# Symmetric transform matrices used as they are, a ring of three modulation tiles, and weight-gradient copies on one engine, in a spectral block's forward and backward pass

## The chip, the cores and the metric

The kernel runs on one core of a Trainium2 chip. A core has TensorE (PE in the profile; PEld is its weight load), VectorE (DVE), ScalarE (ACT), GpSimd (POOL) and SyncE (SP), each with an instruction queue of its own, and 16 DMA engines that all queues share. The metric is device microseconds of the whole execution, the median of several runs. A second, profiled execution gives the busy times and waits. In it, "SPq" and "POOLq" are the instructions with which SyncE and GpSimd start DMA transfers.

## The reference

One token sequence x of 2048 rows and 1024 columns passes two residual branches, each scaled and shifted by a modulation vector computed from a conditioning vector c. All outputs of the forward pass and of its gradient are wanted, ten arrays in all.

```
mod = (silu(c) @ w_mod).reshape(c.shape[0], 6, 1, -1)     # sa, ca, ga, sb, cb, gb
h = layernorm(x) * (1 + ca) + sa
x = x + ga * irfft2(rfft2(h) * (w_r + 1j * w_i))
h = layernorm(x) * (1 + cb) + sb
x = x + gb * (gelu(h @ w1 + b1) @ w2 + b2)
# and the gradients of x, w_r, w_i, w1, b1, w2, b2, c and w_mod for a given grad_out
```

w1 is 1024 by 3584, w2 is 3584 by 1024, and w_mod is 1024 by 6144. All is bfloat16. The gradient of w_mod is an outer product: each 128 by 1024 block of it is one row of the modulation gradient times a column of silu(c). The gradient of c needs the sum of each block of w_mod times that row.

## The kernel before

The two-dimensional transform is done as matmuls with cosine and sine matrices, folded by symmetry into four classes: even and odd cosines (`CE`, `CO`) and even and odd sines (`SE`, `SO`). The matrices are generated once in `gen_mats` and stored in DRAM: `d_SF` for the token axis, `d_E` for the column axis. `spectral_core` does one transform, the multiplication by the weights and the inverse transform. It runs twice, forward and backward (`fwd` is true and false). Its stages are:

- `s_fwd`: four passes with `pu` matmuls along tokens, giving `U`.
- eight pairs (`pair`, L473): `pcs` matmuls along columns, then VectorE products with the frequency weights `ws`, giving `R`. Backward, each pair also writes a piece of the weight gradients (out_2, out_3).
- `s_inv`: `pv` matmuls with the transposed token matrices `smi`, giving `V`.
- `po` matmuls with the transposed column matrices `gm`, whose result goes through `consume`.

The transposed matrices are fetched by transposing DMA transfers from DRAM: `load_smi` (L555) makes eight for each parity of frequency, and L576 to L581 make eight for `gm`. They are started on SyncE's queue during the first three pairs.

Between the two transforms lie the two layers of the mixer. `ph_part` (L661) computes `pp`, the gradient before the activation, and stores it in `d_ph`. `z_block` (L750) handles four 128-row pieces of the hidden layer for one of four token chunks, 28 blocks in all. It loads a piece of `d_ph` into `ph`, computes `pz` with TensorE, moves it out with ScalarE (L767), and runs the chain of the activation and its derivative over the tiles `zb`, `av`, `bv`, `sg`. Two sets of these tiles alternate from block to block (`gts`). The block ends with a multiply that also sums (L784), whose product is stored to `d_gz` (L786). `bo_pass` (L791) multiplies the hidden values by `w2` between the blocks, in an order written out in `plan`, and adds column sums to `gacc` (L825 to L828).

Then comes the gradient through w1 (`pg`, L956) with two layernorm backward steps, and the backward transform. Beside the backward transform TensorE computes the weight gradients. `pieces` (L1072) is a generator: each step is 16 matmuls for a 128 by 512 block (`gw2acc` for w2, `gw1acc` for w1) and a copy of the PSUM block into `gwo` or `gwo1` (L1054, L1120), then a store. Four `fill(1)` calls stand beside each pair, and others are in `consume_bwd` (L1018). `nc.any.tensor_copy` leaves it to the planner whether ScalarE or VectorE makes the copy.

The modulation gradients (`gmod_steps`, L894) go row by row, eight steps for each of six rows. Each step loads a block of w_mod into `wr`, forms the outer product in `gw` (L899) and stores it, then multiplies and sums `wr` (L901). Row 5 runs in the stage of `pg`, with two load tiles and one store tile. Rows 3 and 4 run beside the backward pairs, with one load tile and one store tile. Rows 2, 1 and 0 run at the end.

`consume_bwd` reloads a part of x (`load_tok`, partly by indirect transfers on GpSimd's queue) and normalizes it with four ScalarE instructions (`norm_act`, L440).

Instructions are traced in the order of the program, and a planner orders each engine's queue by priority and by what it expects to be ready. `tc.high_priority()` moves instructions forward, and `tc.issue_after(x)` keeps those of a block behind x on the same engine. On the chip each queue is worked off in that order, and an instruction at its head that waits holds those behind it.

Of the kernel before, what the change touches and what calls it, by code (L numbers as in the profile page):

```python
# [11 lines left out]
BF16 = mybir.dt.bfloat16  # L12
I32 = mybir.dt.int32
ACT = mybir.ActivationFunctionType
ALU = mybir.AluOpType
AX = mybir.AxisListType

P = 128
S = 2048
D = 1024  # L20
# [15 lines left out]
def kernel(  # L36
# [74 lines left out]
    d_P = dram.tile([8, P, 4 * PW], BF16, name="d_P")  # L111
    d_SF = dram.tile([P, 4, 4, 512], BF16, name="d_SF")
    d_E = dram.tile([P, 2, 8, 256], BF16, name="d_E")
    d_gmod = dram.tile([6 * D], BF16, name="d_gmod")
# [341 lines left out]
    def spectral_core(fwd, fb, sms, em, css, pt, evac_u, evac_c, evac_v, consume, o4tag, pfs=None, fill=lambda n: None, mid=lambda: None, beside=lambda n: None):  # L456
# [97 lines left out]

        def load_smi(par):  # L555
            smi = reg.tile([P, 2, 4, 512], BF16, name="smi", tag=("sma", "smb")[par])
            for t in range(2):
                for i in range(4):
                    with tc.issue_after(ld_in[0].ins):
                        nc.sync.dma_start_transpose(out=smi[:, t, :, i * P:(i + 1) * P], in_=d_SF[:, par + 2 * t, i, :])  # L560
            smis.append(smi)

        pair_load(0)
        for par in range(2):
            for m in range(4):
                if par == 1 and m == 2:
                    s_inv(CE, smis[0])
                    s_inv(SE, smis[0])
                pair(par * 4 + m, par, m)
                if par * 4 + m < 7:  # L570
                    pair_load(par * 4 + m + 1)
                beside(par * 4 + m)
                if par == 0 and m < 2:
                    load_smi(m)
                if par == 0 and m == 2:
                    gm = reg.tile([P, 12, 256], BF16, name="gm", tag="gm")  # L576
                    for cl in range(4):
                        for h in range(2):
                            with tc.issue_after(ld_in[0].ins):
                                nc.sync.dma_start_transpose(out=gm[:, 2 * cl:2 * cl + 2, h * P:(h + 1) * P],  # L580
                                                            in_=d_E[:, 0 if fwd else 1, 2 * cl + h, :])  # L581
        s_inv(CO, smis[1])
# [167 lines left out]
    def z_block(b, g0, g1):  # L750
# [3 lines left out]
        for g in range(g0, g1):  # L754
# [27 lines left out]
            for k in range(4):  # L782
                fc = g * 4 + k
                nc.vector.tensor_tensor_reduce(out=av[:, k, :], in0=ph[:, k, :], in1=av[:, k, :], scale=1.0, scalar=0.0,  # L784
                                               op0=ALU.mult, op1=ALU.add, accum_out=gb1_acc[:, fc, b:b + 1])
            nc.gpsimd.dma_start(out=d_gz_v[:, g * 4:(g + 1) * 4, b * BW:(b + 1) * BW], in_=av)  # L786

# [3 lines left out]
    def bo_pass(b, h):  # L791
# [30 lines left out]
        for i in range(4):  # L822
            with ordered():
                last_pe[0] = nc.tensor.matmul(pa[:], lhsT=ones_bf[:], rhs=go[:, i, :], start=(i == 0), stop=(i == 3))
        if b == 0:  # L825
            nc.vector.tensor_copy(out=gacc[:, cs_], in_=pa[0:1, :])
        else:
            tt(gacc[:, cs_], gacc[:, cs_], pa[0:1, :], ALU.add)  # L828

# [64 lines left out]
    def gmod_steps(r, wrs, gws, gr):  # L894
        nc.sync.dma_start(out=gr, in_=d_gmod[r * D:(r + 1) * D].partition_broadcast(P))
        for jc in range(NDC):
# [6 lines left out]
            yield  # L903

    w1Ts = []
    for g in range(7):
# [15 lines left out]
    gmg = reg.tile([P, 2, D], BF16, name="gmg", tag="sb")  # L922
    early = gmod_steps(5, gmw[:], gmg[:, 0:1], gmg[:, 1, :])
    au = reg.tile([P, 4, D], BF16, name="au", tag="px1")
# [12 lines left out]
    for b in range(NB):  # L937
# [26 lines left out]
        for i in range(4):  # L964
            t = 4 * b + i
            ln_bwd(gn3[:, i, :], sums[:, 0, i:i + 1], n3u[:, i, :], stats[:, 2, 0, t:t + 1], gn3[:, i, :], got[:, 4 + i % 2, :])
        tt(pru, gn3[:], n2u[:], ALU.mult)
        g2, ftmp = gn3, pru
# [5 lines left out]
        for i in range(4):  # L974
            t = 4 * b + i
            nc.vector.tensor_tensor_reduce(out=g2[:, i, :], in0=gn3[:, i, :], in1=opcb_row, scale=1.0, scalar=0.0,
                                           op0=ALU.mult, op1=ALU.add, accum_out=s2c[:, i:i + 1])
            ln_bwd(g2[:, i, :], s2c[:, i:i + 1], n2u[:, i, :], stats[:, 1, 0, t:t + 1], g2[:, i, :], got[:, 4 + i % 2, :])
        tt(g2[:], g2[:], go4, ALU.add)
        nc.gpsimd.dma_start(out=chunk_rows(d_gx1, b), in_=g2[:])  # L980
# [5 lines left out]
        if b < NB - 1:  # L986
            sums3_ga(b, au)
            for _ in range(3):
                next(early, None)

# [15 lines left out]
    pfs = [empf[:, 2048:2048 + 4 * PW].rearrange("p (s r w) -> p s r w", s=2, r=2), pf1[:]]  # L1006
    otl = reg.tile([P, 2 * NT * P + D], BF16, name="otl", tag="ot")
    hht = [reg.tile([P, 2, NT, P], BF16, name=f"hht{k}", tag=f"t{k + 2}") for k in range(2)]
    gmy = otl[:, NT * P:2 * NT * P].rearrange("p (a d) -> p a d", d=D)
    sacc = otl[:, 2 * NT * P:2 * NT * P + D]  # L1010
# [7 lines left out]
    def consume_bwd(i, o4, tmp, tmp2, n1):  # L1018
# [7 lines left out]
        load_tok(n1, A_x, i)  # L1026
        norm_act(n1, n1, 0, i)
        tt(tmp, o4, n1, ALU.mult)
# [8 lines left out]
        store_tok(out_1, o4, i)  # L1037
        fill((6, 6, 8, 8)[i])
        for q in range(4):
# [6 lines left out]
    gwo = reg.tile([P, 2, D], BF16, name="gwo", tag="ph")  # L1046

    def gw2_mm(acc, fc, h, t):
        nc.tensor.matmul(acc[:], lhsT=hh_s[hh_o[fc]][:, t, :], rhs=gBs[t // 4][:, t % 4, h * KH:(h + 1) * KH],  # L1049
                         start=(t == 0), stop=(t == NT - 1))  # L1050

    def gw2_out(acc, fc, h):
        with tc.high_priority():
            nc.any.tensor_copy(out=gwo[:, fc % 2, h * KH:(h + 1) * KH], in_=acc[:])  # L1054
        if h == 1:
            nc.gpsimd.dma_start(out=out_6[fc * P:(fc + 1) * P, :], in_=gwo[:, fc % 2])
# [15 lines left out]
    def pieces():  # L1072
# [36 lines left out]
        for fg in range(F // 512):  # L1109
            if fg < 6:  # L1110
                w1g["ins"] = gw1_load(fg + 1)
            gz2 = w1g["gz"][2 * (fg % 2):2 * (fg % 2) + 2]
            for cch in range(NDC):
                acc = ps_f("gw1acc")
                for t in range(NT):
                    nc.tensor.matmul(acc[:], lhsT=n3ns[t // 4][:, t % 4, cch * P:(cch + 1) * P], rhs=gz2[t // 8][:, t % 8, :],  # L1116
                                     start=(t == 0), stop=(t == NT - 1))
                ob = gwo1[:, (fg * NDC + cch) % 8]
                with tc.high_priority():
                    nc.any.tensor_copy(out=ob, in_=acc[:])  # L1120
                nc.gpsimd.dma_start(out=out_4[cch * P:(cch + 1) * P, fg * 512:(fg + 1) * 512], in_=ob)
                yield
# [25 lines left out]

    rows34 = [gmod_steps(r, gmy[:, 0:1], gmy[:, 1:2], sacc) for r in (3, 4)]
    side = [0]  # L1150

    def beside_bwd(n):
        for k in range(4):
            fill(1)
            if k < (0, 2, 2, 2, 2, 2, 3, 3)[n]:
                with tc.issue_after(hh_in[0].ins):
                    next(rows34[side[0] // NDC])
                side[0] += 1

# [58 lines left out]
```

## Time and profile before

The time is 1582.85 us, the median of 3 runs (1582.29 to 1590.55). The profiled run has a span of 1578.6 us.

| stage (us from start) | TensorE busy | granted clock | DMA share |
|---|---|---|---|
| 348 to 567, hidden blocks, first part | 191.0 of 219 | 0.94 | 0.68 |
| 567 to 817, hidden blocks, second part | 240.7 of 250 | 0.97 | 0.87 |
| 817 to 1044, gradient through w1 | 215.5 of 227 | 0.99 | 0.54 |
| 1133 to 1324, backward pairs | 160.0 of 191 | 0.93 | 0.79 |
| 1324 to 1428, inverse transform and x gradient | 100.9 of 104 | 1.00 | 0.67 |
| 1428 to 1545, weight gradient of w1 | 117.0 of 117 | 1.00 | 0.91 |

A stage's busy time is the time in which an engine had an instruction in work. The granted clock is the share of full speed that TensorE was given. The DMA share is the mean busy share of the 16 DMA engines.

In the lines of the prediction, a line of the timeline has start, duration, engine, line and operation, the tiles written and read, a count, and in brackets the idle time before it and what ended it. A line of the waits names who waited for whom, then microseconds in total, times, and the longest.

### The profile page before, as it was taken

The page shows a single profiled execution, that of the slowest core. Times are in us where ns is not written, and L with a number is a line of the kernel's source. Part 1 is how long each engine was busy: PE and PEld are TensorE (multiplying, and loading weights), DVE is VectorE, ACT ScalarE, POOL GpSimd, SP SyncE. Part 2 cuts the span into 40 slices and gives each one's busy share as a digit, 9 for nine tenths or more (in the row PEclk, how much of TensorE's full clock was granted, in tenths as well). Part 3 has the DMA queues.
Part 4 walks back from the last instruction along what each step waited for, and adds up shares of the span by engine and source line. Part 5 has one row for each costly group of instructions (what it writes and reads, how often), then busy time and mean ns, then how long its engine had stood idle before and what let it go on. Part 6 is the DMA issues. An engine that isn't in the chain of part 4 may idle for free.

```text
span 1578.6 us, 18397 instructions
## 1 busy us (share of the span) xinstructions
PE 1449.7 (92%) x6831; PEld 669.1 (42%) x6831; DVE 1074.5 (68%) x1578; ACT 722.3 (46%) x955; POOL 366.7 (23%) x427
## 2 busy tenths in 40 slices
PE   5989899999797989999899999989979869999998
PEld 2434454444343334444344444434434434444443
DVE  5992869887777787877323977976237556898733
ACT  4756556668565565665111423332522424442211
POOL 5710611101112122212111101312014421322423
PEclk8999999999999999999899999999999989999999
DMA  9961937998475766799955446496379857855996
GB/s 329 294 164 54 241 120 238 252 298 279 163 209 174 214 207 233 217 293 270 312 192 175 141 141 213 112 275 155 77 177 238 204 175 222 215 168 144 264 205 191
DMA packets 372514, 325.33 MB, mean 206 GB/s; under 512 B 224436, under 2 KB 315586, under 8 KB 372297
## 3 DMA queue, kind: packets, MB, share of 16 engines
q1 hardware_dynamic: 338680, 209.81, 51.4%
q0 software_dynamic: 33744, 114.36, 20.8%
q8 instruction: 53, 0.87, 0.2%
q14 instruction: 37, 0.30, 0.1%
HBM read 162.57 MB, written 108.05 MB: 171 GB/s over the span
## 4 chain that ended last, share of the span: by engine, by line
PE 39%; DVE 12%; DMA 7%; issue 6%; ACT 3%; SPq 1%; POOL 1%; POOLq 0%; ACTq 0%; DVEq 0%
PE gw1acc L1116 9%; PE gw2acc L1049 7%; PE pbo L805 7%; PE pg L956 5%; PE pz L764 5%; DVE got L882 2%; PE pu L450 2%; DVE gn3a L887 1%; DMA gB<-in_grad_out_dram 1%; DMA d_gz<-gt 1%; DMA gzh<-d_gz 1%; PE pv L543 1%; DVE gt L172 1%; DVE qb L172 1%; SPq L580 1%
## 5 line engine op out<-in xcount | busy, mean ns | idle before, releaser
L647 PE MATMUL pp<-gBoT,wt 128*128 128x512 bf16 x896 | 200.6, 379 | 2.8 <-DMA wt<-in_B_w_dram 1.9
L1116 PE MATMUL gw1acc<-gzh,n3n 128*128 128x512 bf16 x896 | 196.5, 379 | 1.2 <-DMA gzh<-d_gz 1.2
L956 PE MATMUL pg<-w1T,gzr 128*128 128x512 bf16 x896 | 196.7, 381 | 0.4 <-ACT gn3b L961 0.2
L764 PEld LDWEIGHTS <-w 128*128 128x128 bf16 x896 | 89.6, 100 | 140.7 <-issue 40.2
L956 PEld LDWEIGHTS <-gzr 128*128 128x128 bf16 x896 | 87.9, 98 | 107.9 <-issue 3.4
L1116 PEld LDWEIGHTS <-n3n 128*128 128x128 bf16 x896 | 87.6, 98 | 105.1 <-issue 1.5
L647 PEld LDWEIGHTS <-wt 128*128 128x128 bf16 x896 | 87.4, 98 | 104.9 <-DMA wt<-in_B_w_dram 2.4
L764 PE MATMUL pz<-n3Ta,w 128*128 128x512 bf16 x448 | 102.1, 388 | 16.6 <-ACT gt L767 16.6
L764 PE MATMUL pz<-n3Tb,w 128*128 128x512 bf16 x448 | 105.4, 395 | 11.0 <-ACT gt L767 7.7
L1049 PE MATMUL gw2acc<-gB,hhsA 128*128 128x512 bf16 x448 | 102.0, 384 | 0.0
L805 PEld LDWEIGHTS <-hhA 128*128 128x128 bf16 x608 | 60.1, 100 | 81.2 <-issue 13.7
L767 ACT ACTIVATE gt<-pz,b_col 128x512 bf16<-128x512 f32 x112 | 72.7, 682 | 39.7 <-PE pz L764 39.0
L1054 ACT CAST gwo<-gw2acc 128x512 bf16<-128x512 f32 x53 | 30.1, 583 | 129.5 <-PE gw2acc L1049 78.0
L769 ACT ACTIVATE gt<-gt 128x2048 bf16<-128x2048 bf16 x28 | 53.4, 1908 | 59.9 <-DMA d_gz<-gt 59.5
L1120 ACT CAST gwo<-gw1acc 128x512 bf16<-128x512 f32 x48 | 27.8, 583 | 111.1 <-PE gw1acc L1116 97.2
L172 DVE TENSOR_TENSOR gt<-gt,gt 128x2048 bf16<-128x2048 bf16 x56 | 68.2, 1222 | 14.4 <-ACT gt L775 13.5
L172 DVE TENSOR_TENSOR ct<-ct 128x2048 bf16<-128x2048 bf16 x64 | 76.0, 1219 | 1.3 <-DMA d_n<-ct 0.5
L773 ACT ACTIVATE gt<-gt 128x2048 bf16<-128x2048 bf16 x28 | 53.4, 1910 | 36.1 <-DVE gt L172 36.0
L1049 PEld LDWEIGHTS <-hhsA 128*128 128x128 bf16 x448 | 44.3, 99 | 51.9 <-issue 2.5
L1049 PE MATMUL gw2acc<-gB,hht 128*128 128x512 bf16 x256 | 57.9, 388 | 7.3 <-DVE gB L172 7.3
L1049 PE MATMUL gw2acc<-gB,otl 128*128 128x512 bf16 x192 | 45.5, 395 | 19.5 <-DVE gwo L1054 11.3
L543 PE MATMUL pv<-smi,R 128*128 128x512 bf16 x256 | 58.6, 384 | 4.0 <-DVE R L172 4.0
(306 smaller groups left out, 2538.6 us busy)
## 6 DMA issues: line engine op xcount, KB each, us to landing
d_gz<-gt POOLq DMA_DIRECT2D x28, 512.0 KB, 6.5
gzr<-d_gz SPq DMA_DIRECT2D x28, 512.0 KB, 4.9
wblk<-in_w_mod_dram SPq DMA_DIRECT2D x12, 1024.0 KB, 11.9
d_ph<-pho POOLq DMA_DIRECT2D x21, 512.0 KB, 5.1
out_dram<-otl POOLq DMA_DIRECT2D x40, 256.0 KB, 4.3
d_hh<-hhA POOLq DMA_DIRECT2D x19, 512.0 KB, 4.3
w2sD<-in_B_w_dram SPq DMA_DIRECT2D x14, 512.0 KB, 7.1
hhC<-d_ph SPq DMA_DIRECT2D x14, 512.0 KB, 5.1
```

Of the source, the lines that this page charges most:

```text
L172: return nc.vector.tensor_tensor(out=out, in0=a, in1=b, op=op)
L450: last_pu[0] = nc.tensor.matmul(pu[:], lhsT=fb[:, i, cl, c8 * P:(c8 + 1) * P], rhs=sm[:, i, :], start=(i == 0), stop=(i == 3))
L543: nc.tensor.matmul(pv[:], lhsT=R[:, cl * 4 + m, :, :].rearrange("p x w -> p (x w)")[:, base:base + 255:2], rhs=smi[:, cl // 2, m, :], star ...
L647: last_pe[0] = nc.tensor.matmul(pp[:], lhsT=wt[:, fg % 2, cch, k * P:(k + 1) * P], rhs=gBoT[j][:, cch, :], start=(cch == 0), stop=(cch == ...
L764: last_pe[0] = nc.tensor.matmul(pz[:], lhsT=w1s[g][:, cch, k * P:(k + 1) * P], rhs=n3T[:, cch, :], start=(cch == 0), stop=(cch == NDC - 1))
L767: nc.scalar.activation(out=zb[:, k, :], in_=pz[:], func=ACT.Identity, bias=b1_col[:, fc:fc + 1], scale=1.0)
L769: nc.scalar.activation(out=av, in_=zb, func=ACT.Square)
L773: nc.scalar.activation(out=sg, in_=bv, func=ACT.Sigmoid, scale=2.0 * GK)
L805: last_pe[0] = nc.tensor.matmul(pbs[i][:], lhsT=hh[:, k, i * P:(i + 1) * P], rhs=wp[:, k, :], start=False, stop=(g == 6 and k == 3))
L956: nc.tensor.matmul(pgs[i][:], lhsT=gzt[g][:, k, i * P:(i + 1) * P], rhs=w1Ts[g][:, k, h * KH:(h + 1) * KH], start=(g == 0 and k == 0), sto ...
L1049: nc.tensor.matmul(acc[:], lhsT=hh_s[hh_o[fc]][:, t, :], rhs=gBs[t // 4][:, t % 4, h * KH:(h + 1) * KH], start=(t == 0), stop=(t == NT - 1))
L1116: nc.tensor.matmul(acc[:], lhsT=n3ns[t // 4][:, t % 4, cch * P:(cch + 1) * P], rhs=gz2[t // 8][:, t % 8, :], start=(t == 0), stop=(t == NT ...
```

## The change

It has seven edits.

1. The odd matrices of the token axis and of the column axis are symmetric, so their transposes are themselves. `smi` for odd frequencies is now the matrix already in SBUF (`sms[1]`), and `gm` for `CO` and `SO` is loaded without transposing. The transposed even matrices, fetched in the forward pass, are saved in a new DRAM array `d_SI` and reloaded backward without transposing. The remaining transposes of `gm` are spread over two pairs.
2. In `z_block` the product goes into `ph` and is stored from there, so that `av` is free when the product is formed.
3. The `gacc` copy or add has high priority.
4. `gmod_ring` replaces `gmod_steps` for rows 5, 3 and 4: three tiles in turn, loads two steps ahead. A tile is first multiplied and summed, then overwritten with the outer product and stored.
5. Row 5's steps are spread over the stage of `pg`; the steps of rows 3 and 4 come after the last fills of a pair instead of the first.
6. The PSUM copies of the weight gradients are all on ScalarE.
7. In `consume_bwd` two pieces are traced ahead of the norm of reloaded x, and the norm is kept behind the last PSUM copy traced by then. The number of pieces in all is the same.

```
-        def load_smi(par):
-            smi = reg.tile([P, 2, 4, 512], BF16, name="smi", tag=("sma", "smb")[par])
+        def load_smi():
+            smi = reg.tile([P, 2, 4, 512], BF16, name="smi", tag="sma")
             for t in range(2):
...
+                    if fwd:
+                        for i in range(4):
+                            nc.sync.dma_start_transpose(out=smi[:, t, :, i * P:(i + 1) * P], in_=d_SF[:, 2 * t, i, :])
+                    else:
+                        nc.sync.dma_start(out=smi[:, t], in_=d_SI[:, t])
+            if fwd:
+                nc.gpsimd.dma_start(out=d_SI[:], in_=smi[:])
+            smis.extend((smi, sms[1]))
...
+                    if m == 1:
+                        gm = reg.tile([P, 12, 256], BF16, name="gm", tag="gm")
+                        for cl in (CO, SO):
...
+                                nc.sync.dma_start(out=gm[:, 2 * cl:2 * cl + 2, :], in_=d_E[:, v, 2 * cl:2 * cl + 2, :])
+                    else:
+                        cl = (CE, SE)[m - 2]
...
-                nc.vector.tensor_tensor_reduce(out=av[:, k, :], in0=ph[:, k, :], in1=av[:, k, :], scale=1.0, scalar=0.0,
+                nc.vector.tensor_tensor_reduce(out=ph[:, k, :], in0=ph[:, k, :], in1=av[:, k, :], scale=1.0, scalar=0.0,
...
+        with tc.high_priority():
+            if b == 0:
+                nc.vector.tensor_copy(out=gacc[:, cs_], in_=pa[0:1, :])
...
+        for n, (r, jc) in enumerate(steps):
+            buf = bufs[n % 3]
+            nc.vector.tensor_tensor_reduce(out=buf, in0=buf, in1=gr, scale=1.0, scalar=0.0,
+                                           op0=ALU.mult, op1=ALU.add, accum_out=gu[:, r, jc:jc + 1])
+            nc.vector.tensor_scalar(out=buf, in0=gr, scalar1=u_rt[:, jc:jc + 1], scalar2=None, op0=ALU.mult)
+            nc.gpsimd.dma_start(out=out_9[jc * P:(jc + 1) * P, r * D:(r + 1) * D], in_=buf)
+            if n + 1 < len(steps) and steps[n + 1][0] != r:
+                load_g(steps[n + 1][0])
+            if n + 2 < len(steps):
+                load_w(n + 2)
+            yield
...
         load_tok(n1, A_x, i)
-        norm_act(n1, n1, 0, i)
+        fill(2)
+        with tc.issue_after(gw_ev[0].ins):
+            norm_act(n1, n1, 0, i)
...
-        fill((6, 6, 8, 8)[i])
+        fill((4, 4, 6, 6)[i])
...
-            nc.any.tensor_copy(out=gwo[:, fc % 2, h * KH:(h + 1) * KH], in_=acc[:])
+            gw_ev[0] = nc.scalar.copy(out=gwo[:, fc % 2, h * KH:(h + 1) * KH], in_=acc[:])
...
-                    nc.any.tensor_copy(out=ob, in_=acc[:])
+                    gw_ev[0] = nc.scalar.copy(out=ob, in_=acc[:])
...
-            if k < (0, 2, 2, 2, 2, 2, 3, 3)[n]:
+            if 3 - k < (1, 2, 2, 2, 2, 2, 3, 3)[n]:
```

## The prediction

> **What bounds the kernel now.** I read the busy shares first, then the windows by stage, then TensorE's instructions in order of time, and for each gap the queue of the engine that ended it.
>
> ```profile
> PE 1449.7 (92%) x6831; PEld 669.1 (42%) x6831; DVE 1074.5 (68%) x1578; ACT 722.3 (46%) x955; POOL 366.7 (23%) x427
> ```
>
> TensorE is the bound, so only its idle time, 1578.6 - 1449.7 = 129 us, can be won. Two windows hold half of it (the first pair of numbers is length and TensorE busy):
>
> ```profile
> 348.00:567.00 219.00, 190.99 (x842) 83.54 (x841) 161.94 (x248) 145.25 (x139) 35.00 (x40) 0.94 0.68 214
> 1133.00:1324.00 191.00, 160.04 (x765) 76.22 (x763) 105.14 (x151) 61.09 (x99) 55.70 (x62) 0.93 0.79 200
> ```
>
> 28 us are idle in the first (the GELU blocks of `z_block`) and 31 us in the second (the frequency pairs of the backward transform). The granted clock there, 0.94 and 0.93, is below the 0.97 and 1.00 of the stages that follow them. Gaps in order of time, with what ended them:
>
> ```profile
> 423.52 8.68 PE L764 MATMUL pz<-n3Ta,w 128*128 128x512 bf16 x32 [8.22 <-ACT gt L767]
> 484.58 3.36 PE L764 MATMUL pz<-n3Tb,w 128*128 128x512 bf16 x8 [3.23 <-DVE w2sD L826]
> 566.77 3.55 PE L764 MATMUL pz<-n3Ta,w 128*128 128x512 bf16 x8 [7.21 <-ACT gt L767]
> ...
> 1181.85 8.41 PE L1049 MATMUL gw2acc<-gB,otl 128*128 128x512 bf16 x32 [8.18 <-DMA otl<-d_hh]
> 1230.37 1.86 PE L483 MATMUL pcs<-empf,U 128*128 128x256 bf16 x8 [4.39 <-ACT cs01b L613]
> 1289.75 0.58 PE L1049 MATMUL gw2acc<-gB,otl 128*128 128x512 bf16 x1 [11.31 <-DVE gwo L1054]
> 1293.53 1.86 PE L483 MATMUL pcs<-empf,U 128*128 128x256 bf16 x8 [3.20 <-ACT cs01b L613]
> ```
>
> Behind the first kind, the waits in 348 to 567 show ScalarE's Square (L769) waiting for a store, with the PSUM evictions of L767 queued behind it:
>
> ```profile
> ACT gt L769 <- DMA d_gz<-gt: 57.2, 10, 14.0
> PE pz L764 <- ACT gt L767: 24.3, 5, 8.2
> ```
>
> Behind the second kind lie three queues. SyncE issues eight transposes of `gm` ahead of the `d_hh` transpose that TensorE needs; the norm of reloaded x stands on ScalarE for 22 us with three `gwo` copies behind it; VectorE stands in the modulation steps for their load and their store (waits in 1133 to 1324):
>
> ```profile
> 1165.40 11.97 SPq L580 DMA_TRANSPOSE gm<-d_E  x8
> 1177.47 2.10 SPq L1074 DMA_TRANSPOSE otl<-d_hh  x1
> ```
> ```profile
> 1286.78 4.63 ACT L440 ACTIVATE xt<-xt,stats 128x1024 bf16<-128x1024 bf16 x4 [22.04 <-DMA xt<-in_A_x_dram,xu]
> 1291.33 1.52 ACT L1054 CAST gwo<-gw2acc 128x512 bf16<-128x512 f32 x3
> ```
> ```profile
> DVE otl L901 <- DMA otl<-in_w_mod_dram: 39.4, 8, 10.9
> DVE otl L899 <- DMA out_dram<-otl: 24.2, 8, 5.6
> ACT gwo L1054 <- DMA out_dram<-gwo: 45.7, 8, 9.9
> ```
>
> **What the Trainium skill says.** "TensorE: Matmul & The Clock Gate", section "Architectural detail": ScalarE and VectorE are strict first-in-first-out. The trace agrees: the `gwo` copy of 0.69 us that ends the 11.31 us gap runs at 1289.01, only after three L899 ahead of it have waited 4.14, 2.68 and 2.70 us for stores. The same page, "HAM oscillation": a gap beyond about 3.4 us lowers the matmul clock, so a gap costs more than its length. The trace agrees: after the 8.18 us gap 32 matmuls take 8.41 us against 7.07 us elsewhere. "DMA: Bandwidth & Descriptors", section "DMA Transpose (X-bar)": the plain transposing DMA can be issued from SyncE or ScalarE only. Here all are on SyncE, at a median of 1.27 us of its time for an `smi` piece and 1.24 for a `gm` piece, against 0.4 us for a plain load.
>
> **The change part by part.** Line numbers are those of the kernel before.
>
> *GELU product in place (L784 to L786).* `d_gz` is now stored from `ph` and not from `av`. Square, the first write of `av` in block n+2, then waits for block n's VectorE reduction and no longer for its store. One block read off: the reduction ends at 406.2, the store is issued at 406.56, Square starts at 413.90, so it moves 7.7 us earlier. At 566.77: reduction done 539.7, Square 547.07, 7.4 us. At 495.14: 482.7, so 12 us. Each is at least about its gap. The chain of two blocks (Square at 495.1 and 500.9, the second reduction done at 518.9, next Square 521.1) has a period of 26 us; without the store in it about 18 us. TensorE needs 2 x 6.9 us of `pz` and four or more passes of 3.45 us beside them, about 28 us, so it is the bound again. Added: the load of `ph` now waits for the store, some 6.5 us landing after issue. `ph` is needed at the reduction, some 18 us after Square, and load and store together are about 12.5 us, so it is hidden. But the load waits at the head of SyncE's queue, with the `w2` loads (L800) behind it. Those have room: 587.94 issued, used at 605.76, landing 7.1. The wait costs between 0 and 6 us for each of 26 blocks that catches a `w2` load short; I take 5 us in all.
>
> *High priority for the `gacc` add (L826).* Removes the 3.23 us gap at 484.58; one answer.
>
> The seven gaps between 394 and 567 (1.16, 8.22, 0.45, 3.23, 4.33, 3.41, 7.21) make 28.0 us. The slow matmuls after them, against 7.07 for 32, 5.34 for 24 and 1.89 for 8, add 1.6 + 1.5 + 1.7 + 2.7 + 1.7 = 9.2. Of 37 us I take 26: less 5 for the `w2` loads and 6 for what the earlier chain does not cover.
>
> *Symmetric matrices.* Forward: of 24 transposes 12 stay, plus two plain loads and a 1 MB store on GpSimd's queue; backward: 16 `smi` transposes become two plain loads of 512 KB, 8 of `gm` become 4 and two plain loads, spread over two pairs. SyncE time saved backward: 20 x 1.25 - 4 x 0.4 = 23 us, forward 12 x 1.3 = 15 us. On the path this is the 8.18 gap with its 1.3 us of slow matmuls. Forward, `pp` matmuls fill TensorE and only the gap of 3.99 us at 184.13 (waiting for `R`, behind the `ws` loads that those transposes delay) is at stake: 3 us. The added store runs where nothing waits for it until the backward pass: nothing.
>
> *Ring of three tiles.* Loads run two steps ahead and VectorE never waits for a store; its 39.4 + 24.2 us of waits shrink, and with them GpSimd's waits for L899 (40.2 us), behind which the `gwo` stores stand. VectorE work per pair is about 9.4 us plus two steps of 1.7, against TensorE's 4 x 3.45 + 2 = 16, so VectorE is not the bound. Added: a load waits on SyncE for the store of the step before, 2.7 us landing by the DMA table, up to 8 when GpSimd's queue holds it, and the next `d_hh` transpose is behind it. That transpose has two groups of 6.9 us less 5.7 landing, 8 us of room. Bounds: 0 to 8 us for each of 14 loads; I take 4 us in all.
>
> *All copies on ScalarE, norm behind one of them.* Three `gw2` and eight `gw1` copies move: 11 x 0.58 us on an engine that is 46% busy. The norm goes behind two more pieces, past the stage where its load was late: the 11.31 and 3.20 gaps go. VectorE, 93% busy from 1326 to 1428, loses 0.69 us per copy. The norm then starts 6.9 us after `po`, while VectorE has 9.5 us of unfolding to do, and the column sum comes 20.7 us after `po`: nothing.
>
> What stays: copies waiting for their own `gwo` store (45.7 us; two slots as before) and the 2.15 and 4.39 us gaps it makes, in part.
>
> Backward: 8.18 + 0.71 + 2.15 + 4.39 + 11.31 + 3.20 = 29.9 us of gaps, plus 6.0 of slow matmuls, 36 in all. Less 4 for the ring and 6 for the `gwo` slots: 26.
>
> *Sum:* 26 + 26 + 3 = 55, hence 1582.85 - 55 = 1528. Row 5's ring works in a stage that is 95% busy, and the last window is not touched: 0. Estimates of several queues at once lean high, so I take 51: **1532 us**.
>
> **The rivals.**
>
> *A: the backward stage fills again* (15%). Loads waiting at the head of SyncE take the place of the transposes, and DMA, 0.79 busy there, leaves little slack. For: `gwo` copies waiting for stores keep 45.7 us. Against: 20 transposes leave the queues. Only 6 of 26 is won: 26 + 6 + 3 = 35 less, 1548; with 5 us of longer landings 1553.
>
> *B: the GELU stage stays* (10%). The `ph` load's wait moves SyncE's 144.6 us of waiting for L784 onto the store, and `w2` loads starve TensorE. For: a `w2sC` load already costs 4.13 us at 785.30. Against: 18 us between issue and use. 5 + 26 + 3 less: 1549.
>
> *C: no change* (5%): both at once, 3 to 8 us won, 1577.
>
> *D: slower* (8%). The instruction order is planned anew, and a wait of 8 us in front of `d_hh` transposes exceeds their room in some of the 14 steps, say five by 4 us, and `w2` loads in five of 26 blocks by 3 us, with no gain on either side: +35, less 20 regained from the norm and `gm`: 1598.
>
> **How the numbers follow.** The forecast has 62%; A 15, B 10, C 5, D 8. Faster: 62 + 15 + 10 = 87%. Low end: everything returned, 37 + 36 + 4 = 77 less, is 1506; I put it at 1508. High end: A and B lie inside, and half of C and D has to stay out: 1562.
>
> **What would show it.** In the profile after, L769 should wait for VectorE and no longer for `d_gz`, and the waits of L764 on L767 fall from 24.3 to under 6 us. The transposes of `smi` and `gm` fall from 48 to 16. No VectorE wait for an `out_9` store should be left in the pairs, and TensorE should have no gap over 5 us from the start of the pairs to the first `po`. The forecast is wrong if SyncE's waits for stores turn up as TensorE gaps ended by `d_hh` or `w2` loads, or if the plan moves evictions behind other waiting work.

## The result, and the profile after

The changed kernel takes 1526.36 us, the median of 4 runs (1520.35 to 1533.02), against 1584.53 us for the kernel before in the same comparison. The ratio is 0.9628, with a 95% interval from 0.9578 to 0.9678. The profiled spans are 1578.6 and 1525.9 us, so 52.7 us have to be found.

I cut both traces at the same milestones of TensorE: the first `pz` matmul, the first `pg`, the first `gw2acc`, the first backward `pcs`, and the end of the last backward `pv`. The lengths in us:

| kernel | forward | hidden blocks | `pg` | `pu`, first `gw2` | backward pairs | rest |
|---|---|---|---|---|---|---|
| before | 347.1 | 469.9 | 217.3 | 97.7 | 191.6 | 255.0 |
| changed | 350.0 | 430.2 | 217.3 | 99.8 | 168.1 | 260.5 |
| difference | +2.9 | -39.7 | 0 | +2.1 | -23.5 | +5.5 |

The busy shares of the changed kernel first. TensorE does the same 6831 matmuls in 6.6 us less busy time, and as its idle time falls from 129 to 83 us its share goes from 92% to 95%:

```profile
PE 1443.1 (95%) x6831; PEld 669.5 (44%) x6831; DVE 1065.9 (70%) x1565; ACT 729.3 (48%) x968; POOL 363.0 (24%) x428
```

The windows of hidden blocks, pairs and rest, before and then after. The columns are length, busy time of TensorE, of its weight loads, of VectorE, ScalarE and GpSimd (in brackets the instructions), granted clock, DMA share and GB/s:

```profile
347.10:817.00 469.90, 432.56 (x1922) 189.76 (x1921) 322.09 (x481) 270.10 (x256) 84.78 (x92) 0.96 0.78 234
1132.00:1323.60 191.60, 160.64 (x769) 76.72 (x768) 105.14 (x151) 61.71 (x99) 55.70 (x62) 0.93 0.79 200
1323.60:1578.60 255.00, 244.70 (x1188) 115.85 (x1186) 176.34 (x263) 76.62 (x104) 72.84 (x100) 1.00 0.76 195
```
```profile
350.00:780.20 430.20, 418.21 (x1923) 186.75 (x1922) 320.37 (x482) 269.64 (x256) 85.78 (x92) 1.00 0.86 257
1097.30:1265.40 168.10, 158.16 (x769) 75.91 (x768) 104.79 (x150) 57.68 (x96) 55.00 (x62) 0.98 0.87 222
1265.40:1525.90 260.50, 247.54 (x1188) 117.50 (x1186) 170.00 (x252) 87.11 (x119) 68.06 (x100) 0.98 0.75 189
```

Length less busy time is TensorE's idle time. In the hidden blocks it falls from 37.3 to 12.0 us, and the same matmuls take 14.4 us less at a granted clock of 1.00 where it was 0.96. In the pairs idle time falls from 31.0 to 9.9 us and busy time by 2.5. In the rest both grow, by 2.7 and 2.8 us, at a clock of 0.98 where it was 1.00. The page of the Trainium skill that the prediction drew on, "TensorE: Matmul & The Clock Gate", section "HAM oscillation", says that idle gaps beyond about 3.4 us lower the matmul clock. These windows agree that a gap costs more than its length: where gaps went, busy time went with them. They do not agree on the limit. Behind two gaps of the rest, of 3.20 and 2.40 us (shown below), the clock stands at half for 3.4 us (same columns, changed kernel):

```profile
1339.00:1342.40 3.40, 3.40 (x17) 2.11 (x15) 0.86 (x2) 1.20 (x3) 0.00 (x0) 0.50 1.06 342
1383.40:1386.80 3.40, 3.40 (x16) 2.12 (x15) 0.80 (x2) 1.17 (x2) 0.78 (x1) 0.50 0.36 139
```

In the clock records of the 14 profiles from 340 us on, such a stretch begins in the gap or within 3.5 us of its end for 59 of 61 gaps above 3.4 us, for 28 of 36 between 2.4 and 3.4 us, and for 2 of 73 between 0.8 and 1.2 us.

In the hidden blocks the waits of the changed kernel show what became of the chain behind `d_gz`. L779 is the eviction (L767 before), L781 the Square (L769 before):

```profile
ACT gt L781 <- DVE gb_acc L796: 6.9, 4, 4.2
PE pz L776 <- DVE w2sD L839: 1.5, 1, 1.5
PE pz L776 <- ACT gt L779: 1.1, 1, 1.1
```

Square no longer waits for a store, and the 24.3 us that TensorE waited for the eviction are 1.1. What was added shows in SyncE's own queue, before and then after. The load of `ph` is L758 before and L770 after, where the trace calls its two slots w2sA and hhC after an earlier use; the `w2` load is L800 and L812:

```profile
SPq L758 <- DVE gb_acc L784: 144.6, 22, 20.7
SPq L800 <- PE pbo L805: 66.4, 21, 10.3
```
```profile
SPq L770 <- DMA d_gz<-w2sA: 77.8, 12, 12.8
SPq L770 <- DMA d_gz<-hhC: 69.9, 11, 14.7
SPq L812 <- PE pbo L817: 40.1, 18, 10.0
```

The load of `ph` waited for the reduction before; now it waits for the store, 147.7 us in all where it was 144.6. So the queue hardly stands longer. The `w2` loads behind it still wait 40.1 us for a tile to come free (66.4 before), and TensorE waits 3.7 us for them in all where it waited 4.1. So they are not late.

In the pairs these gaps of TensorE above 1 us are left, and the last two lines are those of the rest (timeline of the changed kernel, with other instructions between them left out):

```profile
1148.93 1.21 PE L484 MATMUL pcs<-empf,U 128*128 128x256 bf16 x8 [1.96 <-ACT cs01b L625]
1167.91 1.63 PE L484 MATMUL pcs<-empf,U 128*128 128x256 bf16 x8 [3.09 <-ACT cs01b L625]
1186.75 1.21 PE L484 MATMUL pcs<-empf,U 128*128 128x256 bf16 x8 [1.38 <-ACT cs01b L625]
1205.57 13.94 PE L544 MATMUL pv<-smi,R 128*128 128x512 bf16 x56 [2.19 <-ACT V L622]
...
1337.46 0.60 PE L609 MATMUL po<-gm,V 128*128 128x256 bf16 x4 [3.20 <-ACT ct L612]
...
1381.97 1.03 PE L609 MATMUL po<-gm,V 128*128 128x256 bf16 x8 [2.40 <-DVE ct L612]
```

The 8.18 and 11.31 us gaps are gone. In the rest the kernel before had one of 2.29 us where 3.20 stands now, and one of 1.24 us at 1546.46. The gap of 3.09 us goes back through three queues. ScalarE first, then GpSimd (POOL):

```profile
1166.16 1.07 ACT L1099 CAST gwo<-gw2acc 128x512 bf16<-128x512 f32 x2 [8.65 <-DMA out_dram<-gwo]
1167.12 2.22 ACT L625 CAST cs01b<-pcs 128x512 bf16<-128x512 f32 x3
```
```profile
1159.59 1.48 POOL L531 DMA_INDIRECT out_dram<-empf,xu  x1 [10.65 <-DVE otl L936]
1161.38 0.98 POOL L531 DMA_INDIRECT out_dram<-empf,xu  x1 [0.30 <-issue]
1162.36 0.58 POOL L937 DMA_DIRECT2D out_dram<-otl  x1
1162.94 0.58 POOL L1101 DMA_DIRECT2D out_dram<-gwo  x1
```

The copy at 1166.16 had to wait until the store of its slot had landed. That store was issued at 1162.94, behind an indirect store at whose place GpSimd had stood for 10.65 us. The eviction of `pcs` stands behind the copy, and TensorE has its 3.09 us gap at 1167.91.

### The profile page after: what moved, and what is told of

It is laid out like the page before. It is cut to its first block, busy times and chain, and to the rows that moved or that the text cites. A ratio compares the mean times of both kernels' runs of the same rounds, so it can differ in the third digit from the quotient of the medians.

```text
span 1525.9 us, 18364 instructions
## 1 busy us (share of the span) xinstructions
PE 1443.1 (95%) x6831; PEld 669.5 (44%) x6831; DVE 1065.9 (70%) x1565; ACT 729.3 (48%) x968; POOL 363.0 (24%) x428
## 5 line engine op out<-in xcount | busy, mean ns | idle before, releaser
L776 PE MATMUL pz<-n3Tb,w 128*128 128x512 bf16 x448 | 99.1, 379 | 1.5 <-DVE w2sD L839 1.5
L776 PE MATMUL pz<-n3Ta,w 128*128 128x512 bf16 x448 | 98.6, 379 | 1.1 <-ACT gt L779 1.1
L1165 ACT CAST gwo<-gw1acc 128x512 bf16<-128x512 f32 x56 | 32.6, 583 | 119.4 <-PE gw1acc L1161 110.5
L779 ACT ACTIVATE gt<-pz,b_col 128x512 bf16<-128x512 f32 x112 | 72.9, 684 | 29.1 <-PE pz L776 28.7
L785 ACT ACTIVATE gt<-gt 128x2048 bf16<-128x2048 bf16 x28 | 53.4, 1910 | 64.6 <-DVE gt L173 64.6
L781 ACT ACTIVATE gt<-gt 128x2048 bf16<-128x2048 bf16 x28 | 53.5, 1910 | 7.6 <-DVE gb_acc L796 6.9
L787 ACT ACTIVATE gt<-gt 128x2048 bf16<-128x2048 bf16 x28 | 53.3, 1909 | 0.4
L1166 POOL DMA_DIRECT2D out_dram<-gwo x56 | 30.4, 545 | 81.6 <-ACT gwo L1165 69.0
```

What stands on the lines that cost most here:

```text
L776: last_pe[0] = nc.tensor.matmul(pz[:], lhsT=w1s[g][:, cch, k * P:(k + 1) * P], rhs=n3T[:, cch, :], start=(cch == 0), stop=(cch == NDC - 1))
L779: nc.scalar.activation(out=zb[:, k, :], in_=pz[:], func=ACT.Identity, bias=b1_col[:, fc:fc + 1], scale=1.0)
L781: nc.scalar.activation(out=av, in_=zb, func=ACT.Square)
L785: nc.scalar.activation(out=sg, in_=bv, func=ACT.Sigmoid, scale=2.0 * GK)
L787: nc.scalar.activation(out=bv, in_=bv, func=ACT.Sigmoid, scale=-2.0 * GK)
```

## The experiments

In each table the stages are those of above: hidden blocks, pairs, rest. A profile is one execution. The five timed runs of the changed kernel on one chip spread from 1515.37 to 1528.24 us, and its two profiles differ by 2.3 us in the hidden blocks, 0.7 in the pairs and 0.1 in the rest. So a difference of 2 us in one stage of one profile says nothing.

### One edit at a time on the kernel before

Four kernels, each with one part of the change (edit 3 comes further down). The in-place product is edit 2 alone:

```
-  ...tensor_tensor_reduce(out=av[:, k, :], in0=ph[:, k, :], in1=av[:, k, :], ...
+  ...tensor_tensor_reduce(out=ph[:, k, :], in0=ph[:, k, :], in1=av[:, k, :], ...
-  nc.gpsimd.dma_start(out=d_gz_v[...], in_=av)
+  nc.gpsimd.dma_start(out=d_gz_v[...], in_=ph)
```

> The kernel before with one edit: the GELU product is formed in the tile that held the loaded gradient and is stored from there. Theory: the store stood in the chain of Square, and the whole gain of the hidden blocks comes from this edit; that stage (469.9 us before, 430.2 in the changed kernel) falls to 431 to 437, with only the 3.2 us gap of the column sum left of the seven, and the total to about 1548. Rival: the stage needs the high priority of the column sum as well, or the planner's new order from the other edits; then it stays above 450 us and the total above 1563.

The symmetric matrices are edit 1 alone:

```
-  nc.sync.dma_start_transpose(out=smi[:, t, :, i * P:(i + 1) * P], in_=d_SF[:, par + 2 * t, i, :])
+  nc.sync.dma_start(out=smi[:, t], in_=d_SI[:, t])        # backward
+  smis.extend((smi, sms[1]))
```

> The kernel before with the symmetric matrices alone (fewer transposing transfers, the array of saved transposes). Theory: the 8.2 us gap behind the eight transposes of the column matrices goes and nothing else, so the pair stage falls from 191.6 to about 182 and the total by 9 to about 1575; forward nothing. Rival: VectorE's waits for modulation loads and the late norm hold the pairs at the same pace anyway, so the gap reappears elsewhere: 1582 to 1585.

The ring of three tiles is edits 4 and 5 alone:

```
-  rows34 = [gmod_steps(r, gmy[:, 0:1], gmy[:, 1:2], sacc) for r in (3, 4)]
+  rows34 = gmod_ring((3, 4), gmy, sacc)
```

> The kernel before with the ring of three modulation tiles alone (rows 5, 3 and 4, and the new places of their steps). Theory: VectorE's waits for loads and stores of these rows (39 and 24 us in the pairs) go, but the transposes and the late norm on ScalarE still stop TensorE; of 31 us of gaps in the pairs 7 to 10 go, total about 1574. Rival: GpSimd's queue, free of stores that wait for VectorE, starts the gathers of x early enough for the norm, so the 11.3 and 3.2 us gaps go with this edit alone: pair stage under 176 us, total about 1566.

The copies and the norm are edits 6 and 7 alone:

```
-  nc.any.tensor_copy(out=gwo[...], in_=acc[:])
+  gw_ev[0] = nc.scalar.copy(out=gwo[...], in_=acc[:])
...
-  norm_act(n1, n1, 0, i)
+  fill(2)
+  with tc.issue_after(gw_ev[0].ins):
+      norm_act(n1, n1, 0, i)
```

> The kernel before with the weight-gradient copies all on ScalarE and the norm behind one of them, two pieces later. Theory: the 11.3 and 3.2 us gaps and their slow matmuls go, 16 us in the pairs, and the last stage (255.0 us before, 260.5 in the changed kernel) grows by about 5, because ScalarE's later layernorm work now stands in front of the copies of the next columns; total about 1573. Rival: the last stage's 5 us have another cause and do not show here; total about 1568.

Measured against the kernel before on the same chip:

| kernel | time, us | ratio (95%) | hidden | pairs | rest |
|---|---|---|---|---|---|
| in-place product | 1552.86 | 0.9795 (0.9741 to 0.9848) | 434.0 | 193.0 | 255.5 |
| symmetric matrices | 1572.6 | 0.9920 (0.9893 to 0.9947) | 470.5 | 183.3 | 255.8 |
| ring of three | 1572.95 | 0.9929 (0.9906 to 0.9952) | 469.0 | 178.2 | 254.1 |
| copies and norm | 1585.43 | 1.0004 (0.9984 to 1.0024) | 465.9 | 189.2 | 259.3 |

The product of the four ratios is 0.9651, the whole change 0.9628, so the parts nearly add up. The first two went as expected. For the ring the time came out where the theory had it, but the mechanism is the rival's: the 11.31 us gap in front of `gw2acc` and the 3.20 us gap behind it are gone with the ring alone, and no gap above 2.3 us is left in the pairs after 1220. In the three other kernels of this section that keep the old steps and the copies, the large gap stays, with 13.10 us (product in place), 12.02 (symmetric matrices) and 12.75 (product and `gacc`). With the ring GpSimd starts the gather of x 3.3 us after the last `cs01b` copy ahead of it, where it was 18.7 us, and the norm waits 6.71 us for it on ScalarE, where it waited 22.04:

```profile
1280.39 2.37 ACT L440 ACTIVATE xt<-xt,stats 128x1024 bf16<-128x1024 bf16 x2 [6.71 <-DMA xt<-in_A_x_dram,xu]
```

This kernel has the three tiles and the later place of the steps (edit 5) together. Which of the two removes the gap was not tried.

For copies and norm the theory fell: nothing is won. Its timeline of VectorE, then its gap of TensorE:

```profile
1280.18 0.49 DVE L899 TENSOR_SCALAR otl<-otl,u_rt 128x1024 bf16<-128x1024 bf16 x1 [3.60 <-DMA out_dram<-otl]
1283.35 0.49 DVE L899 TENSOR_SCALAR otl<-otl,u_rt 128x1024 bf16<-128x1024 bf16 x1 [2.68 <-DMA out_dram<-otl]
1286.53 0.48 DVE L899 TENSOR_SCALAR otl<-otl,u_rt 128x1024 bf16<-128x1024 bf16 x1 [2.69 <-DMA out_dram<-otl]
```
```profile
1305.75 16.03 PE L543 MATMUL pv<-smi,R 128*128 128x512 bf16 x60 [11.16 <-DVE R L172]
```

With no copy on VectorE and the norm out of the way, VectorE still stands three times for the store of the one `gw` tile, the products of the last pair come late, and TensorE waits 11.16 us for `R` where it waited 11.31 us for a copy. The wait had been VectorE's all along. The copy was only what TensorE happened to need first, and the norm was late because its gather stood on GpSimd behind stores that wait for VectorE (6.09 and 2.63 us for L899 in the kernel before). So the ring, not the copies or the norm, removes it. The rest of 259.3 us, against 255.0, points to these edits as the source of the changed kernel's longer last stage.

The whole gain of the hidden blocks was tried with edits 2 and 3 together, the product in place and the priority of the `gacc` add:

```
-        if b == 0:
-            nc.vector.tensor_copy(out=gacc[:, cs_], in_=pa[0:1, :])
+        with tc.high_priority():
+            if b == 0:
+                nc.vector.tensor_copy(out=gacc[:, cs_], in_=pa[0:1, :])
```

> The kernel before with the product in place and the high priority of the gacc add. Theory (the two edits make the whole gain of the hidden blocks): hidden blocks 429 to 431 us, where the product in place alone gave 434.0, and the time about 1545 to 1549 us. Rival (the priority is worth nothing and the last 4 us come from the edits elsewhere): hidden blocks 433 to 435 us, time 1551 to 1554 us.

It took 1542.62 us, ratio 0.9781 (0.9766 to 0.9796), with hidden blocks of 430.9 us. This is the changed kernel's 430.2 (432.5 in its second profile), and the two edits make the whole gain of that stage. The time lies below the expected numbers because the kernel before took only 1577.84 us on that chip; by the ratio it would be 1548 us beside 1582.85. The part of the priority, 3.1 us between two profiles, is not shown: the gap that it aims at fell only from 3.72 us in the kernel with the product alone to 1.46, the eight profiles with the changed kernel's code of that stage spread from 428.6 to 432.5 us, and the time intervals of the two kernels overlap.

### What edits 6 and 7 are worth in the changed kernel

First the changed kernel without both (the copies of `gwo1` likewise, and the later `fill` longer by two again):

```
-            gw_ev[0] = nc.scalar.copy(out=gwo[...], in_=acc[:])
+            nc.any.tensor_copy(out=gwo[...], in_=acc[:])
...
-        fill(2)
-        with tc.issue_after(gw_ev[0].ins):
-            norm_act(n1, n1, 0, i)
+        norm_act(n1, n1, 0, i)
```

> The changed kernel without the edits of the copies and of the norm: copies placed by the planner again, norm of reloaded x in front of the two pieces. Theory (the ring alone had removed the 11.3 and 3.2 us gaps, and the copy and norm edits alone lengthened the last stage by 4.3 us): pairs 166 to 171 us, last stage 255 to 256.5 where the changed kernel has 260.5, time about 1522 us. Rival (the prediction's: the norm has to go behind two more pieces or its 11.3 us come back): pairs 175 us or more, time 1530 us or more.

Then with the norm ahead of the two pieces again, all copies still on ScalarE:

```
-        fill(2)
         with tc.issue_after(gw_ev[0].ins):
             norm_act(n1, n1, 0, i)
...
-        fill((4, 4, 6, 6)[i])
+        fill((6, 6, 8, 8)[i])
```

> The changed kernel with all copies still on ScalarE, but the norm of reloaded x traced in front of the two pieces as before. Theory: what lengthens the last stage is that the norm, and with it VectorE's chain of consume_bwd, starts two pieces (13.8 us of TensorE) later, so that VectorE falls behind at the po blocks; then the last stage is 255 to 257 us and the time about 1522 us. Rival: the pinned gw1 copies on ScalarE stand in front of the po copies; then the last stage stays at 259 to 261 us and the time at 1526 us.

Then with only the `gw1` copies given back to the planner, twice:

```
-                    gw_ev[0] = nc.scalar.copy(out=ob, in_=acc[:])
+                    nc.any.tensor_copy(out=ob, in_=acc[:])
```

> The changed kernel with the copies of gw1 placed by the planner again, the norm left two pieces later. Theory (the norm's place costs the 5 us): last stage 259 to 261 us, time 1526 us. Rival (the pinned gw1 copies cost it): last stage 255 to 257 us, time about 1522 us.

> The changed kernel with the planner's gw1 copies once more: if its 4 us in the last stage are a gain in time, 1520 to 1524 us, and below the changed kernel by 3 to 5 us; if not, within 2 us of it.

And the changed kernel itself beside the second of these:

> The changed kernel once more, beside the others on the same chip: 1524 to 1529 us. If the version with the planner's gw1 copies (1522.4 us) is a gain, this stays at least 2 us above it.

| kernel | time, us | ratio (95%) | pairs | rest |
|---|---|---|---|---|
| without edits 6 and 7 | 1527.25 | 0.9649 (0.9628 to 0.9671) | 172.3 | 256.1 |
| norm ahead of the pieces | 1527.6 | 0.9660 (0.9643 to 0.9677) | 168.7 | 260.6 |
| planner's `gw1` copies | 1522.38 | 0.9641 (0.9614 to 0.9667) | 168.8 | 256.7 |
| the same again | 1522.02 | 0.9648 (0.9635 to 0.9661) | 166.1 | 255.9 |
| changed kernel again | 1521.63 | 0.9640 (0.9617 to 0.9664) | 168.8 | 260.4 |

The place of the norm costs nothing and brings nothing: pairs and rest are those of the changed kernel. My theory that its later start lengthens the rest fell. The pinned `gw1` copies go with it: the five profiles with them (the changed kernel twice, copies and norm alone, norm ahead, and the first with moved `gwo` stores below) have 259.3 to 260.6 us there, and the nine that leave them to the planner 254.1 to 257.2. How, the third `po` block shows. VectorE of the changed kernel, then of the kernel with the planner's `gw1` copies:

```profile
1379.03 2.29 DVE L173 TENSOR_TENSOR ct<-ct,xt 128x4096 bf16<-128x4096 bf16 x1 [4.56 <-DMA xt<-d_gx]
1381.24 0.68 DVE L612 CAST ct<-po 128x512 bf16<-128x512 f32 x1
```
```profile
1375.41 0.69 DVE L612 CAST ct<-po 128x512 bf16<-128x512 f32 x1 [2.85 <-PE po L609]
1379.43 2.29 DVE L173 TENSOR_TENSOR ct<-ct,xt 128x4096 bf16<-128x4096 bf16 x1 [3.33 <-DMA xt<-d_gx]
```

With every `gw1` copy on ScalarE the planner orders VectorE's queue anew. The `po` copy stands behind an addition that waits 4.56 us for its load, and TensorE has the gap of 2.40 us at 1381.97. With the planner's copies it stands ahead, and that gap is not there. All five profiles with pinned `gw1` copies have a gap of 2.3 to 2.6 us at this place, each followed by 3.41 us of half clock, and none of the nine others has it. Gap and half clock make some 4 us (an estimate: 2.4 us and half of 3.41), which is about the difference of the stage. In the pairs the `gw2` copies on ScalarE are worth some 4 us by one profile (172.3 against 166.1 to 168.8). In the time nothing is left of edits 6 and 7 together.

The version with the planner's `gw1` copies has the shorter rest in both profiles, but beside the changed kernel on the same chip its time is not lower, 1522.02 against 1521.63. The expectation of 3 to 5 us less was a miss. Of the five runs of each, the profiled one was the slowest of the changed kernel (1528.24) and the fastest of the other (1517.13). The 95% intervals of the two ratios are some 4 and 2 us wide to each side, so these runs neither show a gain of 4 us nor rule it out.

### The stores of gwo on another queue

The remaining gaps of the pairs come from `gwo` stores that stand on GpSimd's queue. So they were started on ScalarE's:

```
-            nc.gpsimd.dma_start(out=out_6[fc * P:(fc + 1) * P, :], in_=gwo[:, fc % 2])
+            nc.scalar.dma_start(out=out_6[fc * P:(fc + 1) * P, :], in_=gwo[:, fc % 2])
```

> The changed kernel with the stores of gwo started on ScalarE's queue instead of GpSimd's, where they stand behind gathers and scatters that wait for other stores. Theory: ScalarE's waits of 5.7 to 8.7 us for these stores and the four gaps of TensorE that follow them (1.96, 3.09, 1.38, 2.19 us) go; pairs 168 down to 159 to 163 us, time 1518 to 1521 us. Rival: the two slots of gwo with a store of several us in flight still make the copy wait, or the store waits for nothing but delays ScalarE by its issue; pairs 166 to 169 us, time 1524 to 1527 us.

It took 1534.73 us, ratio 0.9705 (0.9681 to 0.9730), with pairs of 174.8 us: slower than the changed kernel, which neither theory nor rival had. The waits of the copies for these stores did go, from 39.6 to 3.8 us, and so did the gaps that they made. But a new gap of 11.96 us came, in front of a `pv` matmul, and VectorE's queue shows why:

```profile
1208.32 1.23 DVE L934 CUSTOM_DVE_ANT_0 otl<-otl 128x1024 bf16<-128x1024 bf16 x1 [2.12 <-DMA otl<-in_w_mod_dram]
...
1211.46 0.68 DVE L622 CAST V<-pv 128x512 bf16<-128x512 f32 x1
```

The planner had put this one `V` copy on VectorE, behind a modulation step that waited for its load. The next kernel keeps all `V` copies of the backward transform on ScalarE as well, and gives back the `gw1` copies:

```
-    ...new_pair_temps(["t0", "t1", "t2", "t3"]), act_copy, s_copy, act_copy, consume_bwd, ...
+    ...new_pair_temps(["t0", "t1", "t2", "t3"]), act_copy, s_copy, s_copy, consume_bwd, ...
```

> The changed kernel with three edits: gw1 copies placed by the planner again, gwo stores started on ScalarE's queue, and all V copies of the backward transform on ScalarE. Theory (the 11.96 us gap came from one V copy that the planner had put on VectorE behind a modulation step that waited for its load; without it the stores on ScalarE's queue win what the waits for gwo stores cost): pairs 160 to 165 us, last stage 256 to 257 us, time 1511 to 1517 us. Rival (the stores on ScalarE's queue cost the pairs by themselves): pairs 169 us or more, time 1521 us or more.

It took 1521.09 us, ratio 0.9633 (0.9620 to 0.9646), with pairs of 170.5 and a rest of 255.1 us. The rest is as short as expected; for the pairs and the time the rival held. ScalarE's timeline (ACTq is the start of a store), then a gap of TensorE:

```profile
1179.38 1.34 ACT L625 CAST cs01b<-pcs 128x512 bf16<-128x512 f32 x2
1190.22 0.34 ACTq L1101 DMA_DIRECT2D out_dram<-gwo  x1
1190.60 1.34 ACT L625 CAST cs01b<-pcs 128x512 bf16<-128x512 f32 x2 [9.88 <-DMA otl<-d_hh]
...
1205.55 0.34 ACTq L1101 DMA_DIRECT2D out_dram<-gwo  x1
1205.93 1.07 ACT L625 CAST V<-pv 128x512 bf16<-128x512 f32 x2 [6.35 <-DMA ws<-in_A_w_i_dram]
```
```profile
1206.57 4.00 PE L544 MATMUL pv<-smi,R 128*128 128x512 bf16 x9 [5.56 <-ACT V L625]
```

ScalarE does no work from 1180.7 to 1190.6. The store is issued at 1190.22, and the trace puts the wait down to a `d_hh` transpose on SyncE's queue, whose data the store does not use. Similar waits of 6.35 and 5.21 us name `ws` and `gm` loads. The semaphores in the trace tell why. The landing of each transfer is counted on a semaphore, and the transfers of SyncE and ScalarE use the same eight in turn. The store at 1190.22 is counted on the one on which the `d_hh` transpose was counted, which SyncE had started at 1182.83, and it is not issued until that transpose has landed, at 1190.14. The same holds for 11 of the 16 `gwo` stores of these pairs: each is issued within 0.1 us of the landing of the transfer that had its semaphore last, one that SyncE had started. The stores on GpSimd's queue use eight other semaphores, and no `gwo` store of the changed kernel's pairs has such a wait. So on ScalarE the store holds up the evictions that TensorE needs; the 5.56 us gap is one case. No kernel tried is measurably faster than the changed one.

## Why the prediction was right

The forecast was 1532 us and the runs gave 1526.36, inside its range. Its sum before the reserve was 26 + 26 + 3 = 55 us; the span fell by 52.7. But the terms are not all right, and that the sum came out is in part luck: 13.7 us more than forecast in the hidden blocks stand against 16.0 less in the other stages.

- **Hidden blocks: 26 forecast, 39.7 measured.** The mechanism held: Square waits for the reduction, 24.3 us of waits became 1.1. Mis-sized were three terms. "5 for the `w2` loads" was nothing: TensorE's waits for `w2` loads were 4.1 us before and are 1.6 + 1.4 + 0.7 = 3.7. "6 for what the earlier chain does not cover" was nothing as well, since no gap of `pz` behind an eviction is above 1.2 us. And 9.2 us for slow matmuls, counted only behind the seven gaps, were 14.4 over the stage. Of these some come and go: the second profile of the changed kernel has two stretches of half clock there that the first has not.
- **Pairs: 26 forecast, 23.5 measured.** Gaps won were 21.0 us against 19.9 in the sum. Slow matmuls were 2.5 us instead of 6.0, as the clock is 0.98 and not 1.00. The symmetric matrices alone gave 8.3 us of the 9.5 put down to them.
- **Copies and norm: the step that failed.** "The 11.31 and 3.20 gaps go" with the norm behind two more pieces: alone it moved the gap onto `R` (11.16 us), while the ring alone (with its steps in their later place) removed both. In the pairs the ring, in the sum a cost of 4 us, won 13.4 alone, and copies and norm won 2.4. I had read VectorE's three waits for the store ahead of the copy, and still gave the gap to the norm and the copy. That the total held was luck: the ring was in the same change, and the sum counted the gaps once for the stage.
- **"Its 39.4 + 24.2 us of waits shrink."** Less than half of that: the 24.2 us for the store went, but the loads still cost 36.9 us of 39.4, and `d_gmod` 6.1 of 9.7. These waits lie on VectorE, which has room, and in the gaps followed here they reach TensorE only through GpSimd's queue and the `gwo` slots.
- **Forward: 3 forecast, none found.** The transposes did leave SyncE, but TensorE's gap for `R` is 4.40 us where it was 3.99. "Behind the `ws` loads that those transposes delay" was a wrong reading. SyncE's `ws` load behind the transposes had landed at 174.8. VectorE waited for the `ws` load on GpSimd's queue, an indirect load that stands there 11.3 us in both kernels (before, with VectorE's wait for it, and then after):

```profile
163.94 11.28 POOL L469 DMA_INDIRECT ws<-in_A_w_r_dram,xu  x1 [2.45 <-DVE qa L172]
177.40 1.23 DVE L172 TENSOR_TENSOR qa<-Pt,ws 128x2052 bf16<-128x2052 bf16 x1 [3.06 <-DMA ws<-in_A_w_r_dram,xu]
```
```profile
166.07 11.27 POOL L470 DMA_INDIRECT ws<-in_A_w_r_dram,xu  x1 [2.45 <-DVE qa L173]
```

The +2.9 us of the stage can't be told from nothing: nine profiles with the changed kernel's forward code lie between 345.5 and 350.0 us, the five with the code before between 347.1 and 350.7. In the one shown, the first 87 us have a clock of 0.90 where before has 0.94.

- **Last stage: "the last window is not touched", 0 forecast, +5.5 measured.** The pinned `gw1` copies reorder VectorE's queue there, which makes the 2.40 us gap and the half clock after it. I had costed the copies by their 0.58 us, not by what the planner would do.

Of what the prediction wanted to see, the transposes of `smi` and `gm` are 16, VectorE has no wait for an `out_9` store in the pairs, and no gap there is above 5 us. Rival A, loads at the head of SyncE filling the pairs again, did not come: no `d_hh` gap above 1 us is left. Rival B had its premise: the wait did move onto the store (144.6 to 147.7 us). It cost nothing, because the `w2` loads behind it still waited for tiles, not for their turn. In the stage of `pu` the same 410 matmuls take 1.8 us longer, at a clock of 0.95 where it was 0.97. This is not the change: the stage is 97.7 us long in the profile before, but 99.9 with edit 2 alone and 100.7 with edits 2 and 3, whose code there is that of the kernel before.

## What to carry to other kernels

A wait in a queue belongs to the first instruction that stands in it, not to the one the starved engine names; take away the second alone and the gap reappears under another name, as 11.31 us became 11.16. When a store is moved to another tile, the wait moves to whatever writes that tile next; whether that costs anything is read from the queue behind it, and here the `w2` loads behind it were waiting for tiles anyway. An edit that pins copies to one engine has to be costed in every stage in which those copies run, with the new order of the other engine's queue. And before a store is moved to another engine's queue, look what that queue's stores wait for: here it was transfers whose data they do not use.

## What the hardware showed that was not expected

- One indirect load of `ws` on GpSimd, always the same one of the forward pass, stood for 11.27 to 11.28 us in each of the 14 profiles, where the other 31 of each took 0.9 to 2.7 us. Why is open. Spans on GpSimd are rough.
- A store started from ScalarE's queue, whose data the engine itself had just written, was issued only when a transfer of another queue had landed: 9.88 us for a `d_hh` transpose, 6.35 us for a `ws` load. It waited for the transfer that had its completion semaphore before it.
- The clock fell to half for 3.41 us after gaps of 2.4 to 3.4 us in 28 of 36 cases.
